# A one-core attention and feed-forward kernel: another prologue, a last group in halves, a second attention buffer and a new written-out order

## The chip, the cores and the metric

The kernel runs on one core of a Trainium2 chip. The metric is the device time of one execution in microseconds (us). A core has five engines with instruction streams of their own: TensorE (PE; its weight loads are listed as PEld), VectorE (DVE), ScalarE (ACT), GpSimd (POOL) and SyncE (SP, which here only issues DMAs). Matmul results land in PSUM, eight banks of 128 partitions by 512 f32 values; everything else is in SBUF.

## What is computed

`x` has 2048 tokens of 640 features. After a layernorm without weights, multi-query attention (32 heads of size 20 that share one key and one value head) and a feed-forward block of width 1728 run on the same normalised input, and both results are added to `x`.

```python
def _A_ref(x, wq, wk, wv, wo):
    q = (lambda x, *d: x.transpose(*d))((x @ wq).reshape(B, S, H, Dh), 0, 2, 1, 3)
    k = x @ wk
    v = x @ wv
    scores = jnp.einsum("bhqd,bkd->bhqk", q, k) * (Dh ** -0.5)
    p = _softmax(scores, axis=-1)
    o = jnp.einsum("bhqk,bkd->bhqd", p, v)
    return (lambda x, *d: x.transpose(*d))(o, 0, 2, 1, 3).reshape(B, S, H * Dh) @ wo

def _B_ref(x, w1, w2):
    h = jnp.einsum("bsd,df->bsf", x, w1)
    h = _silu(h)
    out = jnp.einsum("bsf,fd->bsd", h, w2)
    return out

x = A_x
xn = _layernorm(x, axis=-1)
return x + _A_ref(xn, A_wq, A_wk, A_wv, A_wo) + _B_ref(xn, B_w1, B_w2)
```

## The kernel before, in words

**A planner writes the order.** While the program is built, a class `Sched` (from L170) keeps a modelled clock per engine and commits operations in the order in which they would become ready (`ready` L229, `commit` L254, `run` L279), with priorities for the operations of ACT, DVE, POOL and SP. The result is one fixed in-order list per engine, with semaphores between them; on the chip nothing is reordered. So a constant of the planner (`T_PE`, `SWITCH`, `t_mm` L401 and the like) costs no time itself, but another value gives another order.

**Score blocks.** The work is cut into 2048 score blocks: one 128-token key tile, one head, one chunk of 512 query tokens. There are 4 chunks; a group is 4 heads of one chunk, 64 blocks, 32 groups in all. A block's matmul uses 32 of the 128 rows, so blocks of up to four heads stand side by side in the array. TensorE visits the scores in runs ("S visits", `do_S` L1122, matmul L1152) of mostly three or four blocks, each block into a PSUM bank of its own. The exponential of a block is taken on ScalarE (L1180, one instruction for one to three neighbouring banks) or, for about a third of the blocks, approximated on VectorE by clamped integer arithmetic (`p1` L1197) and two phase-shifted copies, made by VectorE (L1225) or GpSimd (L1231); such a block is then multiplied by three value matrices. The second product ("PV", `do_pv` L1047, matmul L1062) fills one bank, 7, with 32 columns for each of the four heads, four 32-column matmuls to a pass of 512.

**Jobs.** Between score visits and PV passes stand passes of other work: the queries of later heads and chunks (`qd_job` L1313, evicted at L1329 and spread to 32-row slots by 20-row DMAs, L1338), the hidden layer (`h_job` L1350, ACT L1375, DVE L1383) and the output projections (`out_job` L1425). They and PV use the same column-tiled form (`cols` L520, matmul L522); changing between it and a score visit is a change of the array's tiling. Where the planner finds TensorE idle it may put in matmuls of zeros (`fill` L911, matmuls L929 to L952).

**The order around the change.** The first 64 blocks are ordered by the planner's rules (`step` L728); from there the string `ORDER` (L76) says what TensorE does next: `P` a PV pass, `J` a pass of a job, and a letter of `VISITS` a score visit of so many blocks, so many of them for VectorE. What remains after the last score goes by `tail` (L794).

**Prologue** (`prologue`, from L1572). x comes in 16 tiles of 128 tokens on SP's queue (L1588), then the weights; `wk` and `wv` on ACT's queue (L1602). Statistics are taken by VectorE (L1693, L1695) or, for `ACT_STATS`, by ScalarE's accumulator (L1678, L1681). The reciprocal root is a Newton iteration on VectorE (`newton` L1722, L1733 to L1751) in the batches of tiles (0,4), (4,10), (10,16). `norm` (L1711) then applies it on the engine listed. Tiles 0 to 3, 7 and 8 are transposed on TensorE (`tr_job` L1800, matmul L1804; evicted by ACT L1812 or DVE L1815), the ten tiles of `DT` by DMA from SP's queue (L1772). `k_job` (L1819, eviction L1831, shifted copy on POOL L1833) and `v_job` (L1838, three scaled copies L1852) make keys and values for every four tiles; `q_job` (L1290) makes the queries of the first heads for all 512 tokens of chunk 0 in five matmuls (L1295), evicted by ACT at L1303. ScalarE also copies three weights into padded slots (L1664 and twice L1667). A DMA of constants (L1784) fills the offset planes that the queries of the other heads need first.

**End of a group** (`end_group` L1271). VectorE evicts bank 7 (L1274), DMAs transpose it, VectorE takes the reciprocal of the sums (L1258), GpSimd normalises (L1263). When a chunk's heads are there, `try_oT` (L1390) issues DMA transposes into the one buffer `oT`, from which the output jobs read; this waits until the outputs of the chunk before have been evicted. The last group is transposed on TensorE in one piece (L1282, L1411). Of the last chunk's eight output tiles (4 token tiles by 2 halves of 320 columns), four have their first terms summed early and evicted as f32 (`yx`, L1457); for the other four `hold_job` (L1498) keeps the partial sum, with the residual added by multiplying with an identity, in a bank, so that ScalarE can evict the final sum (L1468). VectorE evicts the others with the addition (L1471); the result leaves by DMA (L1475).

## Time and profile before

| | us |
|---|---|
| runs of the kernel before | 683.64, 685.71, 685.64 (median 685.64) |
| the profiled execution, its own time | 685.26 |
| span of that execution in the profile | 683.4 |

The mean clock that TensorE was granted is 0.998 of full speed. The page lists, for each engine, busy time and its share of the span, then the chain of work that ended last, followed back from the last instruction to what released it, then the costliest groups of instructions by line, engine and operation. In a row of the timeline stand start, length, engine, line and operation, output and input with partitions and elements, the number of instructions in the row, and in brackets how long the engine had been idle and what ended that. A row of several instructions covers them all. Matmuls overlap in the pipeline, so a pass costs the distance from one start to the next and not the length shown.

### The profile page before, as it was taken

The numbers are of one execution on the slowest core, as the hardware profiler recorded it, in microseconds if no ns is written. First come the engines' busy times: TensorE is split into PE (matmuls) and PEld (weight loads), VectorE is DVE, ScalarE is ACT, GpSimd is POOL, SyncE is SP. The second block draws the span as 40 slices with busy tenths as digits, with TensorE's granted clock in tenths as the row PEclk, the third lists the DMA queues.
The fourth block names the chain that finished last, engine by engine and source line by source line (L and its number), as shares of the span: only waits on it lengthen the run. The fifth ranks groups of instructions, "written<-read, shape, count | busy, mean of one in ns | idle before, by whom it ended". The sixth has DMA issues, their size and how long they took to land.

```text
span 683.4 us, 22606 instructions
## 1 busy us (share of the span) xinstructions
PE 668.2 (98%) x9667; PEld 228.3 (33%) x9667; DVE 622.1 (91%) x1115; ACT 663.8 (97%) x756; POOL 552.7 (81%) x436
## 2 busy tenths in 40 slices
PE   7899999999999999999999999999999999999997
PEld 3332323333333333333333333333333333333324
DVE  7889989889999989899899999999999999999985
ACT  5999999999999999999999999999999999999995
POOL 3477899987888998898888987878879787788882
PEclk9999999999999999999999999999999999999999
DMA  9546210000021000111112000010112000000012
GB/s 273 149 143 209 65 19 10 11 18 18 17 36 29 10 18 17 29 36 17 30 29 41 13 23 17 29 30 18 29 30 48 9 3 19 19 10 19 20 23 58
DMA packets 52568, 28.00 MB, mean 41 GB/s; under 512 B 38422, under 2 KB 51830, under 8 KB 52470
## 3 DMA queue, kind: packets, MB, share of 16 engines
q1 hardware_dynamic: 51014, 26.35, 15.0%
q8 instruction: 78, 1.28, 0.8%
q10 hardware_dynamic: 1456, 0.22, 0.2%
q14 instruction: 20, 0.16, 0.1%
HBM read 11.44 MB, written 2.62 MB: 21 GB/s over the span
## 4 chain that ended last, share of the span: by engine, by line
PE 86%; DVE 5%; ACT 5%; DMA 3%; issue 1%; SPq 0%; POOL 0%; ACTq 0%
PE psall L1062 30%; PE psall L1152 28%; PE psall L522 27%; ACT sbt L1180 4%; DVE sbt L1197 3%; DMA sbt<-sbt 2%; DMA sbt<-in_A_x_dram 1%; ACT sbt L1713 0%; DVE sbt L1225 0%; DVE sbt L1383 0%; PE psall L1362 0%; PE psall L1295 0%; DVE sbt L1693 0%; PE psall L1804 0%; DVE sbt L1274 0%
## 5 line engine op out<-in xcount | busy, mean ns | idle before, releaser
L1180 ACT ACTIVATE sbt<-psall 128x1024 bf16<-128x1024 f32 (+2 forms) x670 | 627.1, 1040 | 4.1 <-PE psall L1152 3.0
L1231 POOL TENSOR_TENSOR sbt<-sbt 128x768 int32<-128x768 int32 (+1 forms) x368 | 518.6, 1433 | 95.0 <-DVE sbt L1225 82.2
L1197 DVE TENSOR_SCALAR sbt<-psall 128x512 int16<-128x512 f32 x710 | 465.7, 685 | 41.9 <-PE psall L1152 34.9
L1062 PE MATMUL psall<-sbt 128*32 128x512 bf16 x3468 | 279.3, 383 | 0.4 <-DVE sbt L1274 0.4
L1152 PE MATMUL psall<-sbt 32*128 32x512 bf16 x2048 | 252.9, 384 | 4.9 <-DVE sbt L1197 2.2
L522 PE MATMUL psall<-sbt 128*32 128x320 bf16 (+1 forms) x3879 | 235.1, 331 | 1.4 <-DMA sbt<-sbt 1.1
L1152 PEld LDWEIGHTS psall<-sbt 32*128 32x128 bf16 x2048 | 65.5, 91 | 238.2 <-issue 89.0
L522 PEld LDWEIGHTS psall<-sbt 128*32 128x32 bf16 x3879 | 86.7, 95 | 89.4 <-issue 44.0
L1062 PEld LDWEIGHTS psall<-sbt 128*32 128x32 bf16 x3468 | 71.2, 95 | 102.6 <-issue 71.2
L1225 DVE TENSOR_SCALAR sbt<-sbt 128x1536 int16<-128x1536 int16 (+1 forms) x118 | 66.3, 566 | 0.4
L1383 DVE SCALAR_TENSOR_TENSOR sbt<-sbt,psall 128x512 bf16<-128x512 bf16 (+1 forms) x56 | 37.8, 675 | 0.4 <-ACT sbt L1375 0.3
L1375 ACT ACTIVATE sbt<-psall 128x512 bf16<-128x512 f32 x54 | 33.2, 616 | 0.6
L1263 POOL TENSOR_TENSOR sbt<-sbt 128x320 bf16<-128x320 bf16 x31 | 22.5, 727 | 5.3 <-DVE sbt L1225 3.5
L1274 DVE CAST sbt<-psall 128x512 bf16<-128x512 f32 x32 | 21.8, 682 | 0.2 <-PE psall L1062 0.2
L952 PE MATMUL psall<-sbt 128*128 128x512 bf16 (+2 forms) x46 | 13.0, 426 | 1.8 <-DVE sbt L1632 1.2
L1471 DVE SCALAR_TENSOR_TENSOR sbt<-psall,sbt 128x320 bf16<-128x320 f32 x28 | 13.4, 486 | 0.9 <-PE psall L522 0.7
L1833 POOL TENSOR_SCALAR sbt<-sbt 128x256 bf16<-128x256 bf16 x8 | 3.8, 476 | 12.2 <-DVE sbt L1831 11.6
L1329 DVE TENSOR_SCALAR sbt<-psall 128x512 bf16<-128x512 f32 (+1 forms) x19 | 13.0, 683 | 0.3
L1693 DVE BATCH_NORM_STATS2 sbt<-sbt 128x6 f32<-128x320 bf16 x24 | 10.7, 470 | 2.4 <-DMA sbt<-in_A_x_dram 2.4
L1718 POOL TENSOR_SCALAR sbt<-sbt 128x640 bf16<-128x640 bf16 x5 | 4.3, 872 | 7.6 <-DVE sbt L1718 5.4
L1258 DVE RECIPROCAL sbt<-sbt 128x16 f32<-128x16 bf16 x31 | 7.6, 246 | 2.7 <-DMA sbt<-sbt 2.6
L952 PEld LDWEIGHTS psall<-sbt 128*128 128x128 bf16 x46 | 4.5, 108 | 7.8 <-issue 2.4
(70 smaller groups left out, 87.9 us busy)
## 6 DMA issues: line engine op xcount, KB each, us to landing
sbt<-in_A_x_dram SPq DMA_DIRECT2D x32, 160.0 KB, 3.7
out_dram<-sbt SPq DMA_DIRECT2D x15, 160.0 KB, 1.8
sbt<-in_B_w_dram SPq DMA_DIRECT2D x5, 432.0 KB, 6.3
sbt<-sbt SPq DMA_DIRECT2D x105, 20.0 KB
sbt<-in_B_w_dram SPq DMA_DIRECT2D x13, 160.0 KB, 3.0
sbt<-sbt SPq DMA_DIRECT2D x1, 1024.0 KB, 6.4
sbt<-sbt SPq DMA_TRANSPOSE x57, 2.5
sbt<-in_A_wo_dram SPq DMA_DIRECT2D x5, 160.0 KB, 3.0
```

The lines of the kernel that those rows point to most:

```text
L522: ins = pe.matmul(self.bk(b, 0, n, j, j + SLOT), w[:, j:j + SLOT], x, start=start, stop=stop, tile_position=(0, j), skip_group_check=True)
L952: return pe.matmul(self.bk(b, 0, n), self.zero[:, 0:P], self.zero[:, 0:n], start=True, stop=True)
L1062: ins = pe.matmul(self.bk(UBANK, 0, QW, r, r + SLOT), self.v[:, it.w, it.kt, :], it.x(), start=f, stop=False, tile_position=(0, r), skip_g ...
L1152: ins = pe.matmul(self.bk(bank[i]), self.kT[r:r + SLOT, 1 if i in dv else 0, kt * P:(kt + 1) * P], self.qT[r:r + SLOT, g % 8, (g // 8) % 2 ...
L1180: return a.activation(self.E[:, (b0 + lo) * QW:(b0 + lo + m) * QW], self.ps[:, b * BANK:(b + m) * BANK], AF.Exp, scale=ACT_SCALE)
L1197: return v.tensor_scalar(self.Z[:, zs, zp * QW:(zp + 1) * QW], self.bk(bb), 0.0, ZMAX, ALU.max, ALU.min)
L1225: sc.new("dve", td, lambda v, k=k: v.tensor_scalar(self.Y[:, zs, k, 0:w], self.Z[:, zs, 0:w], float(PH[k + 1][0]), None, ALU.add), zk, yk, ...
L1231: sc.new("pool", tp, lambda v, k=k, cb=cb: v.tensor_tensor(self.Y[:, zs, k, 0:w].bitcast(I32), self.Z[:, zs, 0:w].bitcast(I32), cb, ALU.ad ...
L1263: op = sc.new(eng, 0.75 if eng == "pool" else t_dve_ps(16 * DH), lambda v: v.tensor_tensor(dst, ut[:, :, :, 0:DH], rb, ALU.mult), [key, (" ...
L1274: ev = sc.new("dve", t_dve_ps(QW), lambda v: v.tensor_copy(self.U[:, up, :], self.bk(UBANK)), [("UB",)], [("U", up)], prio=U_PRIO, name=f" ...
L1375: sc.new("act", t_act(QW), lambda a: a.activation(t, src, AF.Tanh, scale=0.5), [("B", b)], [("tb", tp)], prio=X_PRIO, name=f"th{c}_{fk}")
L1383: sc.new("dve", t_dve_ps(QW), lambda v, r0=r0, r1=r1, ht=ht: v.scalar_tensor_tensor(out=ht[r0:r1, :], in0=t[r0:r1, :], scalar=1.0, in1=src ...
```

## The change

It has six parts, and lines of the changed kernel are some 10 to 40 off those of before.

1. **Loads.** x tile 1 is loaded from ACT's queue; `wk` and `wv` from SP's, after tiles 0, 2 and 3.
2. **Statistics and norm.** Tiles 0 and 1, and tiles 2 and 3, form two batches whose root is taken by ScalarE's Sqrt and inverted by VectorE; Exp's table is loaded after the second. Newton stays for the batches (4,9) and (9,16). The norm is (x − mean) · rstd; tiles 0 and 2 are normalised by GpSimd, 1 and 3 by VectorE; one tile less is normalised by ScalarE (3 of 16 instead of 4). The statistics that ScalarE takes are those of tiles 7, 8, 9, 14.
3. **Weights and evictions.** The three padded copies move from ScalarE to GpSimd. The evictions of the transposed tiles 0 to 3 are all VectorE's. The queries of the first heads are made by token tile (`q_part`) and evicted in two halves of 256, one by VectorE and one by ScalarE. A `v_job` is evicted by one instruction for the three scalings. The transposes, k and q parts are issued in the order `HEAD`.
4. **Order.** The planner's constants, the earliest times and priorities of prologue operations (`AT`, `PRI`) and the whole string `ORDER` are new; zero matmuls are allowed at a higher busy share in the first 64 steps. The code that could attach single matmul rows to score visits, which was switched off (`RIDE_MIN = 99`), is gone.
5. **Two attention buffers.** Odd chunks' transposes go to the part of `xnT` that held tokens 0 to 511, so that `try_oT` waits for the chunk before the last.
6. **Last group.** Eviction, transpose, reciprocal, normalisation and second transpose each run in two halves of 256 tokens. All eight last output tiles have their partial sums evicted as f32, `hold_job` is gone; three outputs are copied by ScalarE and added by GpSimd, five are added by VectorE; the last token tile's output leaves in two halves, on SP's and ACT's queues.

```diff
-H0_STEP = 24
+H0_STEP = 30
-NEARLY = 2
+BY_ACT = ((0, 0), (0, 1), (2, 0))
-SWITCH = 0.1
-T_PE = 0.2215
+SWITCH = 0.106
+FIRST = 0.01
+T_PE = 0.2165
...
-    "JJJcJGPCJPPbPPPHPCGPJJhJJBJBPPPPPBPKPcPPePHPPMPfbPPPfPPBbPPmBPPbPPBPJbJPbPJJBJPBPJJBJBJJPbJJJJJPPbBP"
+    "hGPPfPPbPPfPPHhbJJgJJJhgPPPPPfPPbPPFPPBPPckPPbkPcPJgPJBJPcJJPHGPPPFPPaJJJBPJJPBFPJJJCJJaJJJJJghPPPPH"
...
-FILL_EARLY = 0.6
+FILL_EARLY = 0.95
-PRO = "v0 t7 t8 v1 k2 k3 q1 k4 k5 v2 k6 k7 d0 v3"
-ACT_STATS = [4, 8, 9, 14]
-NW_ENG = ("dve", "dve", "dve")
-NORM_ENG = ['pool', 'pool', 'pool', 'act', 'act', 'pool', 'dve', 'act', 'dve', 'pool', 'dve', 'act']
-BATCHES = ((0, 4), (4, 10), (10, 16))
+HEAD = "t1 t0 p0 t2 k0 p1 t3 p2 k1 p3"
+Q_ENG = ['dve', 'act']
+W_ENG = ("pool", "pool", "pool")
+X_ENG = ['dve', 'dve', 'dve', 'dve']
+PRO = "t7 v0 t8 v1 k2 k3 q1 k4 k5 k6 v2 k7 d0 v3"
+ACT_STATS = [7, 8, 9, 14]
+NW_ENG = ['sqrt', 'sqrt', 'dve', 'dve']
+NORM0 = ['pool', 'dve', 'pool', 'dve']
+NORM_ENG = ['dve', 'pool', 'pool', 'act', 'pool', 'pool', 'dve', 'act', 'dve', 'pool', 'dve', 'act']
+BATCHES = [[0, 2], [2, 4], [4, 9], [9, 16]]
...
+        for h in (1, 0):
+            c0 = 256 * h
+            ev = sc.new("dve", t_dve_ps(256), lambda v, c0=c0: v.tensor_copy(
+                self.U[:, up, c0:c0 + 256], self.bk(UBANK, c0, c0 + 256)), [("UB",)], [("Uh", h)],
+                prio=U_PRIO + 0.001 * h, name=f"Uev{g}")
...
+    def q_part(self, i):
...
+        half = i // 2
...
+        for k in range(DC):
+            def f(pe, b, k=k):
+                return pe.matmul(self.bk(b, i % 2 * P, i % 2 * P + P), self.wqp[:, k, 0:P],
+                                 self.xnT[:, k, i * P:i * P + P], start=(k == 0), stop=(k == DC - 1))
...
+    def oT_of(self, c):
+        if c % 2:
+            return self.xnT[:, :, 0:QW], [("xnT", i) for i in range(4)]
+        return self.oT[:, :, :], [("oT", i) for i in range(4)]
...
-        if c < 0 or c in self.oT_made or self.norm_made[c] < need or (c > 0 and self.f_done[c - 1] < 8):
+        if c < 0 or c in self.oT_made or self.norm_made[c] < need or (c > 1 and self.f_done[c - 2] < 8):
...
+            if src == "yx" and (i, e) in BY_ACT:
...
+                op = sc.new("act", t_act(320), lambda a: a.activation(half, ps, AF.Copy, scale=0.5), [("B", b)],
+                            [("half", k)], prio=X_PRIO, name=f"out{n}_{e}")
...
+                sc.new("pool", 0.7, lambda g: g.tensor_tensor(ost[:, e0:e0 + 320], half, in1, ALU.add),
+                       [("half", k), rk], wk, prio=X_PRIO, name=f"add{n}_{e}")
...
-        np_("act", t_act(400), wkrep, [("st", "k")], [("wk",)], prio=1.0, name="wkrep")
+        copy(W_ENG[0], *wkrep(), [("st", "k")], [("wk",)], 1.0, "wkrep")
...
+        load_x(0)
+        load_x(1, "act")
+        load_x(2)
+        load_x(3)
...
-                xa(n), self.xslot(n), self.rstd[:, n:n + 1], self.nb[:, n:n + 1], ALU.mult, ALU.add),
+                xa(n), self.xslot(n), self.mv[:, n, 0:1], self.rstd[:, n:n + 1], ALU.subtract, ALU.mult),
...
+            sq = np_("act", 0.22, lambda v: v.activation(v_, self.mv[:, a:b_, 1], AF.Sqrt, bias=self.eps[:, :]),
+                     mvk(a, b_) + [("eps",)], [("va", a)], prio=-1.0, name="sqrt")
+            np_("dve", 0.16, lambda v: v.reciprocal(self.rstd[:, a:b_], v_), [("va", a)], [("rs", a)], prio=-0.1,
+                name=f"rstd{a}")
```

More of the change, by code (lines that the diff above doesn't have):

```diff
@@ L599, in bank_for_job @@
             banks = [b for b in range(7) if b not in hold]
+        banks = [b for b in banks if b not in self.heldb.values()]
         best = None
@@ L1749, in newton @@
                     nw(lambda v: v.tensor_tensor(y_, w_, y_, ALU.mult), rw + rr, rr)
+            if all(eng_of(n) != "act" for n in range(a, b_)):
+                return
             if eng == "dve":
```

418 lines of the change are left out of this document (204 added, 214 removed).

## Prediction

> **What bounds the kernel now.** I read the page first (busy time per engine, then the chain of work that ended last), then the busy time by stage, then single stretches of the timeline.
>
> ```profile
> span 683.4 us, 22606 instructions
> PE 668.2 (98%) x9667; PEld 228.3 (33%) x9667; DVE 622.1 (91%) x1115; ACT 663.8 (97%) x756; POOL 552.7 (81%) x436
> PE 86%; DVE 5%; ACT 5%; DMA 3%; issue 1%; SPq 0%; POOL 0%; ACTq 0%
> ```
>
> TensorE is busy 98% and carries 86% of the final chain; ScalarE, at 97%, is hardly freer. The stages below are cut at the starts of the first score block, the 16th, the 64th and block 1920 of 2048, and at the last exp's end; columns are stage, length, busy time (instructions) of PE, PEld, DVE, ACT, POOL, then clock, DMA share, GB/s.
>
> ```profile
> 0.00:9.95 9.95, 6.65 (x23) 2.55 (x23) 6.37 (x25) 4.93 (x10) 5.39 (x24) 1.00 0.83 229
> 9.95:15.82 5.87, 5.73 (x43) 3.36 (x44) 4.75 (x19) 3.95 (x8) 0.05 (x1) 0.71 1.03 334
> 15.82:27.46 11.64, 8.71 (x87) 3.97 (x85) 10.86 (x48) 11.54 (x17) 4.34 (x6) 1.00 0.59 184
> 27.46:44.53 17.07, 16.51 (x199) 6.61 (x200) 13.72 (x29) 16.29 (x18) 12.27 (x13) 1.00 0.65 182
> 44.53:632.89 588.36, 585.99 (x8689) 195.20 (x8687) 548.07 (x930) 584.97 (x658) 497.38 (x370) 1.00 0.12 29
> 632.89:673.90 41.01, 38.82 (x497) 12.71 (x493) 34.32 (x60) 40.57 (x45) 33.27 (x25) 1.00 0.11 25
> 673.90:683.40 9.50, 5.78 (x144) 3.93 (x139) 4.01 (x10) 1.53 (x4) 0.00 (x0) 1.00 0.20 71
> ```
>
> Each stage has its own limit: before 15.82 a chain of dependences; to 27.46 ScalarE (11.54 of 11.64); from there TensorE, though in the middle ScalarE lies only 1.0 behind it (584.97 against 585.99); from 632.89 ScalarE (40.57 of 41.01); then a chain again. The profiled run took 685.26, 1.86 more than its span; the median of the runs is 685.64. All sums start from 685.26.
>
> **Prologue to the first score block.**
>
> ```profile
> 1.82 1.28 ACT L1757 ACT_TABLE_LOAD   x1 [1.82 <-issue]
> 3.11 0.20 ACT L1757 ACTIVATE sbt<-sbt 128x1 f32<-128x1 f32 x1
> 3.13 1.28 DVE L1693 BATCH_NORM_STATS2 sbt<-sbt 128x6 f32<-128x320 bf16 x3 [2.01 <-DMA sbt<-in_A_x_dram]
> 6.16 0.54 ACT L1667 ACTIVATE sbt<-sbt 128x400 bf16<-128x400 bf16 x1 [2.13 <-DMA sbt<-in_A_wq_dram]
> 7.34 0.17 DVE L1733 TENSOR_SCALAR sbt<-sbt 128x4 f32<-128x4 f32 x1
> 9.41 1.50 DVE L1718 TENSOR_SCALAR sbt<-sbt 128x640 bf16<-128x640 bf16 x4
> 12.37 2.29 PE L1295 MATMUL psall<-sbt 128*128 128x512 bf16 x5
> 15.82 0.60 PE L1152 MATMUL psall<-sbt 32*128 32x512 bf16 x6
> L1713 ACT ACTIVATE sbt<-sbt 128x640 bf16<-128x640 bf16 x4 | 3.5, 914 | 0.0
> L1833 POOL TENSOR_SCALAR sbt<-sbt 128x256 bf16<-128x256 bf16 x8 | 3.8, 476 | 12.2 <-DVE sbt L1831 11.6 <-DVE sbt L1225 0.5
> ```
>
> Before, all four tiles wait for one Newton chain (7.34 to 9.41), the last norm ends at 10.91, and q waits for four transposes and their evictions until 12.37. After, tiles 0 and 1 need only their own statistics: the three statistics from 3.13 to 4.41 set the pace, so the pair is aggregated near 5.5, and root (the nearest row is the one-element activation of 0.20) and reciprocal, each with its hand-over an estimated 0.4, and VectorE's statistics of tile 2 between them put the first norm's end near 7.3. Norms of tiles 0 and 2 stand on GpSimd behind the two pad copies (nearest row: 476 ns for 256 elements; I take 0.6 each), the second of which waits for the weight that ScalarE picks up at 6.16 today: norm 0 ends near 8.2, norm 2 near 9.2. All four transposed-tile evictions now stand on VectorE among the statistics and half of the q parts; placing these in the built order by their rows, tile 3 is evicted near 12.5, the last q part (640 of 2560 columns, a fourth of 2.29) ends near 13.4 and the first score block starts near 14.4: −1.4. Bounds: −0.4, if the VectorE queue slips by two more evictions, to −2.6, if the Newton chain's 2.07 and half a microsecond behind it go entirely. The new table loads cost nothing here: the first takes the old one's place at 1.82, the second (1.28) lies ahead of ScalarE's first statistics, while ScalarE waits for tiles. Loads moved to other queues cost nothing either, as tile 0 keeps its place.
>
> The Trainium skill, "ScalarE: Activation LUTs", section "What ACT_TABLE_LOAD costs", adds a drain of 1.38 us to the 1.28 us load at each change of set. This trace agrees with the load (1.28); behind it the next activation starts at 3.11, 0.01 after its end, so that no drain is seen there, but nothing ran ahead of it, and a change from one set to another is not in the trace.
>
> **From there to block 64.** ScalarE binds and loses a norm (0.91) and a pad copy (0.54): of these and the start, 1.4 + 0.9 + 0.5 = 2.8 could remain. But the second limit is SP's queue:
>
> ```profile
> 26.31 0.17 DVE L1751 SCALAR_TENSOR_TENSOR sbt<-sbt 128x6 f32<-128x6 f32 x1
> 20.20 14.62 SPq L1772 DMA_TRANSPOSE sbt<-sbt  x10
> 34.86 5.98 DMA sbt<-sbt
> 40.88 0.40 PE psall L522 x4
> ```
>
> Ten transposes issue from 20.20 to 34.82, then comes the copy that fills the offset planes of the other heads, on which TensorE waits until 40.88. The last batch's Newton chain ends at 26.48 and six of the ten stand behind it: 8.3, or 1.4 each. After, the batches (with a three-tile lead) let that chain end near 24.5, an estimate from the 1.4 of the start and the norm that ScalarE loses; but tile 9 has moved into the last batch, so seven transposes follow, 9.7, and the copy issues between 34.2 and 34.6 and lands 0.2 to 0.7 earlier than now (5.98 later). Counted in the two built orders, 61 score blocks instead of 55 stand ahead of the first such score: six at 17.07/48 = 0.36 are 2.1 of work, of which I take 1.3 as done in time, for VectorE too is busy 10.86 of 11.64 in the stage before. So the gain at block 64 lies between 0.2 + 1.3 = 1.5 and 2.8; I take **−2.2**, the middle, which holds the start's 1.4. The q and v edits lie inside it: one VectorE instruction in place of three per v part leaves that engine as busy as now, since it takes two more tile evictions.
>
> **The middle.** Nothing is computed less; the order is rewritten. What an alternation costs:
>
> ```profile
> 299.46 0.73 PE L522 MATMUL psall<-sbt 128*32 128x320 bf16 x16
> 300.12 0.39 PE L1152 MATMUL psall<-sbt 32*128 32x512 bf16 x3
> 300.45 0.61 PE L1062 MATMUL psall<-sbt 128*32 128x512 bf16 x8
> 300.99 0.39 PE L1152 MATMUL psall<-sbt 32*128 32x512 bf16 x3
> 301.31 1.05 PE L1062 MATMUL psall<-sbt 128*32 128x512 bf16 x16
> 302.30 0.40 PE L1152 MATMUL psall<-sbt 32*128 32x512 bf16 x4
> 58.88 0.39 PE L1152 MATMUL psall<-sbt 32*128 32x512 bf16 x4
> 59.66 0.39 PE L1152 MATMUL psall<-sbt 32*128 32x512 bf16 x3 [0.38 <-DVE sbt L1197]
> L1180 ACT ACTIVATE sbt<-psall 128x1024 bf16<-128x1024 f32 x570 | 542.0, 1040 | 3.7 <-PE psall L1152 2.8
> L1180 ACT ACTIVATE sbt<-psall 128x1536 bf16<-128x1536 f32 x49 | 71.9, 1479 | 0.2
> L1180 ACT ACTIVATE sbt<-psall 128x512 bf16<-128x512 f32 x51 | 29.8, 620 | 0.3 <-PE psall L1152 0.2
> PEld psall L1152 <- ACT sbt L1180: 48.0, 119, 1.0
> ```
>
> Start to start, four 512-wide passes with their change of shape take 302.30 − 301.31 = 0.99, two take 0.54, so a pass costs 0.225 and a change 0.09; the score visit adds 0.33: 0.42 per visit, be it of three blocks or four. A 320-wide pass costs (0.66 − 0.09)/4 = 0.14. In the built orders, between blocks 64 and 1920, separate visits fall from 567 to 555 (four-block ones rise from 108 to 131, longer ones from 25 to 28): −12 × 0.42 = −5.0. A visit of seven splits in two halves 0.78 apart (58.88 to 59.66) with a 0.38 wait for VectorE, 0.78 more than one visit: three more cost 3 × 0.78 = +2.3. Two 512-wide and four 320-wide passes less: −0.45 − 0.56. Zero matmuls grow from 448 to 1248 columns: 800/512 × 0.225 = +0.35. Sum **−3.4**. Bounds: −5.7 without the cost of the long visits; on the other side ScalarE, which the order does not relieve: 548 two-block, 60 three-block and 63 one-block exps stand for 570, 49 and 51, at the means quoted −22.9 + 16.3 + 7.4 = +0.8, for one block more in all. The second attention buffer lets output transposes be written sooner, hidden already: TensorE is idle for only 588.36 − 585.99 = 2.4 there.
>
> **The end.**
>
> ```profile
> 674.49 0.68 DVE L1274 CAST sbt<-psall 128x512 bf16<-128x512 f32 x1
> 676.01 0.49 DVE L1263 TENSOR_TENSOR sbt<-psall,sbt 128x320 bf16<-128x320 f32 x1
> 678.40 1.68 DVE L1471 SCALAR_TENSOR_TENSOR sbt<-psall,sbt 128x320 bf16<-128x320 f32 x4 [0.72 <-PE psall L522]
> 679.79 0.44 ACT L1468 ACTIVATE sbt<-psall 128x320 bf16<-128x320 f32 x1 [0.43 <-PE psall L522]
> ```
>
> From 632.89 ScalarE binds and its work stays. From the last group's eviction at 674.49 to the last output eviction's end at 680.23 it is 5.74. In halves, the first half's transposes start some 0.3 sooner, but VectorE then has about 14 instructions: two evictions, two reciprocals, two normalisations (about half of 0.68, 0.26, 0.49 plus fixed parts: 2.0 in all), attention copies and five outputs at 0.42 (1.68/4) and partial sums between them; about 5.95. ScalarE's three outputs go on to GpSimd, beside them. **+0.2**, bounds −1.0 (full overlap of the halves) and +0.8 (one GpSimd add last).
>
> **Sum:** −2.2 − 3.4 + 0.2 = −5.4; 685.26 − 5.4 = **679.9**.
>
> **Rivals.** (a) *ScalarE takes the middle's bound.* It lies 1.0 behind TensorE already; if its 0.8 more counts and TensorE's saving is lost in waits, −2.2 + 0.8 + 0.2 = −1.2: 684.1. For it: the windows row. Against: exps wait for scores by only 2.8 in all, and ScalarE's start is earlier. (b) *The start's gain stops at SP's queue:* the copy lands at 40.8 again and blocks fill no gap; the start's 2.2 falls to zero: 682.1. (c) *The early zero matmuls do not hold the clock*, granted 0.71 in the second stage; PE was busy for 6.65 of the first 9.95, and the built order has 37 zero matmuls instead of 25 ahead of the first score. All q parts at half speed would take their 2.29 as now instead of about 1.1, which I have half counted: +1.2, 681.1. (d) *Slower: the longer visits wait for banks.* A four-block visit needs four free banks, and 24 more of them in the whole kernel (120 to 144) each wait for an exp. Place: score weight loads behind the exps, priced at 48.0/119 = 0.40. 24 × 0.40 = +9.6 on −5.4: 689.5. It wipes the gain out from 5.4/24 = 0.23 per visit, and shows as slower from 0.33. For: that wait is the largest with a real releaser. Against: the timeline at 302.30 shows a four-block visit without a wait.
>
> (e) *The table change drains ScalarE as well.* If its second load costs twice its row, statistics on ScalarE slip by 1.4, and of this about 1.0 reaches block 64: 680.9. That is the Trainium skill's rule named above; by its figure the change would cost 2.66.
>
> **How the numbers follow.** Forecast 0.40; (a) 0.15; (b) 0.15; (c) 0.10; (e) 0.05; (d) 0.15. Runs of this kernel tell about 0.3% from no change, that is 683.6 and 687.7. Forecast, (b), (c) and (e) are faster: 0.70; (a) is within: 0.15; (d) slower: 0.15. The range runs from 676.5 (start −2.8 and middle −5.7, with a tail of +0.2, give 677.0, less the half microsecond by which executions differ, 685.26 and 685.64 being two of them) to 686.0, which takes in (a) with the start's lower bound and the tail's +0.8 (−1.4 + 0.8 + 0.8 = +0.2, 685.5) and the same half microsecond; (d) is left out.
>
> **What would show it.** First score block at 14.4 (right) or near 15.5 (VectorE's queue); block 64 at 42.3; blocks 64 to 1920 in 585.0, with TensorE's waits for exps at 48 as now, where (d) needs 57; if ScalarE's busy time fills the middle while PE's falls, it is (a); a granted clock near 0.7 after 10 us is (c); a gap behind the second table load is (e); 5.9 from the last eviction of the group to the last output eviction. The forecast is wrong if visits saved are paid back by waits, which the total of these waits tells.

## The result, and the profile after

The changed kernel is slower: 693.9 us median (692.96 to 694.83, four runs) against 684.85 for the kernel before in the same sessions; the ratio is 1.0133, 95% interval 1.0110 to 1.0157. The forecast was 679.9, with a range to 686.0. The profiled execution took 693.66, its span is 691.5, and so 8.1 longer than that of before.

The page of the changed kernel, in the order in which the forecast read it:

```profile
span 691.5 us, 22597 instructions
PE 670.0 (97%) x9666; PEld 229.5 (33%) x9669; DVE 624.0 (90%) x1108; ACT 661.7 (96%) x754; POOL 572.8 (83%) x453
PE 72%; ACT 12%; DVE 8%; DMA 4%; POOL 2%; issue 1%; DVEq 0%
PE psall L1033 25%; PE psall L1119 23%; PE psall L527 22%; ACT sbt L1142 12%; DMA sbt<-sbt 4%; DVE sbt L1159 4%; POOL sbt L1715 2%; DVE sbt L1690 1%; DVE sbt L1187 1%; DVE sbt L1237 0%; PE psall L940 0%; DMA sbt<-in_A_x_dram 0%; PE psall L1366 0%; PE psall L1850 0%; DVE sbt L1481 0%
```

Only one engine's busy time grew by much: GpSimd, 552.7 to 572.8; seven norms of 2.50 in place of five of 0.87 are 13.1 of these 20.1. And a line of GpSimd, the norm (L1715), has come into the final chain with 2% of the span, some 14 us. The busy time by stage, with the edges at the same blocks as before (first, 16th, 64th, 1920th, last exp's end). In this table the block edges lie 0.08 ahead of the starts in the timeline; in later tables they lie up to 0.24 beside them, by the same amount at both ends of a stage. The text gives a block's start as the timeline has it:

```profile
0.00:17.29 17.29, 14.16 (x86) 7.20 (x87) 11.69 (x40) 8.43 (x18) 12.47 (x33) 1.00 0.87 253
17.29:33.51 16.22, 10.31 (x92) 4.91 (x92) 10.25 (x46) 11.18 (x15) 10.43 (x5) 0.79 0.39 114
33.51:52.07 18.56, 16.94 (x177) 6.38 (x178) 12.76 (x24) 15.95 (x19) 12.70 (x13) 0.90 0.75 177
52.07:640.15 588.08, 583.04 (x8673) 194.64 (x8669) 547.63 (x927) 583.70 (x660) 499.03 (x374) 1.00 0.12 29
640.15:681.76 41.61, 39.96 (x523) 13.25 (x519) 35.09 (x59) 41.30 (x43) 35.70 (x27) 1.00 0.16 25
681.76:691.50 9.74, 5.59 (x131) 3.17 (x124) 6.57 (x19) 1.09 (x3) 2.51 (x3) 1.00 0.20 69
```

Block 64 comes at 52.15 instead of 44.53: +7.6, nearly the whole loss. In the second row's stage no engine is near its limit (ScalarE leads with 11.18 of 16.22; GpSimd spends 10.43 on five instructions), which is what a chain of waits looks like. From block 64 to 1920 the stage is 0.28 shorter: TensorE is busy 2.95 less, and idle 2.67 more. The rest is +0.5 up to the last exp's end and +0.24 behind it.

Four of the five instructions are norms, the fifth is a pad copy of 0.52. First the norms of before in the view of their line (minimum, median, maximum in ns), then GpSimd's timeline and TensorE's of the changed kernel:

```profile
L1718 POOL TENSOR_SCALAR sbt<-sbt x5: 868/875/875, 19.3 to 28.1; 128x640 bf16<-128x640 bf16 x5
```

```profile
7.79 4.99 POOL L1715 TENSOR_SCALAR sbt<-sbt 128x640 bf16<-128x640 bf16 x2 [0.29 <-DVE sbt L1692]
19.89 4.98 POOL L1715 TENSOR_SCALAR sbt<-sbt 128x640 bf16<-128x640 bf16 x2 [2.70 <-DVE sbt L1715]
25.30 2.50 POOL L1715 TENSOR_SCALAR sbt<-sbt 128x640 bf16<-128x640 bf16 x1
30.89 2.50 POOL L1715 TENSOR_SCALAR sbt<-sbt 128x640 bf16<-128x640 bf16 x1 [3.08 <-DVE sbt L1753]
```

```profile
10.35 0.45 PE L1831 MATMUL psall<-sbt 128*128 128x128 bf16 x5 [1.00 <-POOL sbt L1715]
12.83 0.45 PE L1831 MATMUL psall<-sbt 128*128 128x128 bf16 x5 [0.89 <-POOL sbt L1715]
17.36 0.60 PE L1119 MATMUL psall<-sbt 32*128 32x512 bf16 x6
27.86 0.71 PE L1831 MATMUL psall<-sbt 128*128 128x128 bf16 x5 [4.37 <-POOL sbt L1715]
```

A GpSimd norm takes 2.50 us, where the norm of before took 0.87 on the same 128x640 tile. TensorE's transposes of tiles 0, 2 and 8 wait for it, the last for 4.37; behind that wait, transposes that took 0.44 take 0.71: the clock granted in the stage is 0.79.

### The profile page after: what moved, and what is told of

The parts are those of the page before. It is cut to its first block, busy times and chain, and to the rows that moved or that the text cites. A ratio compares the mean times of both kernels' runs of the same rounds, so it can differ in the third digit from the quotient of the medians.

```text
span 691.5 us, 22597 instructions
## 1 busy us (share of the span) xinstructions
PE 670.0 (97%) x9666; PEld 229.5 (33%) x9669; DVE 624.0 (90%) x1108; ACT 661.7 (96%) x754; POOL 572.8 (83%) x453
## 4 chain that ended last, share of the span: by engine, by line
PE 72%; ACT 12%; DVE 8%; DMA 4%; POOL 2%; issue 1%; DVEq 0%
PE psall L1033 25%; PE psall L1119 23%; PE psall L527 22%; ACT sbt L1142 12%; DMA sbt<-sbt 4%; DVE sbt L1159 4%; POOL sbt L1715 2%; DVE sbt L1690 1%; DVE sbt L1187 1%; DVE sbt L1237 0%; PE psall L940 0%; DMA sbt<-in_A_x_dram 0%; PE psall L1366 0%; PE psall L1850 0%; DVE sbt L1481 0%
## 5 line engine op out<-in xcount | busy, mean ns | idle before, releaser
L1193 POOL TENSOR_TENSOR sbt<-sbt 128x768 int32<-128x768 int32 (+2 forms) x374 | 521.6, 1420 | 91.5 <-DVE sbt L1187 79.2
L1119 PE MATMUL psall<-sbt 32*128 32x512 bf16 x2048 | 250.3, 385 | 6.1 <-DVE sbt L1159 2.3
L527 PE MATMUL psall<-sbt 128*32 128x320 bf16 (+1 forms) x3847 | 231.0, 331 | 1.1 <-DVE sbt L1462 1.1
L527 PEld LDWEIGHTS psall<-sbt 128*32 128x32 bf16 x3847 | 85.2, 95 | 90.6 <-issue 46.0
L1033 PEld LDWEIGHTS psall<-sbt 128*32 128x32 bf16 x3466 | 70.1, 95 | 101.0 <-issue 68.9
L1187 DVE TENSOR_SCALAR sbt<-sbt 128x1536 int16<-128x1536 int16 (+2 forms) x116 | 65.5, 571 | 0.7
L1715 POOL TENSOR_SCALAR sbt<-sbt 128x640 bf16<-128x640 bf16 x7 | 17.5, 2500 | 6.1 <-DVE sbt L1753 3.1
L953 PE MATMUL psall<-sbt 128*128 128x512 bf16 (+5 forms) x56 | 16.6, 440 | 1.7 <-DVE sbt L1624 1.2
L1842 DVE COPY sbt<-psall 128x640 bf16<-128x640 bf16 x6 | 2.9, 487 | 6.8 <-PE psall L1831 6.8
```

Source lines behind the costliest of these rows:

```text
L527: ins = pe.matmul(self.bk(b, 0, n, j, j + SLOT), w[:, j:j + SLOT], x, start=start, stop=stop, tile_position=(0, j), skip_group_check=True)
L1033: ins = pe.matmul(self.bk(UBANK, 0, QW, r, r + SLOT), self.v[:, it.w, it.kt, :], it.x(), start=f, stop=False, tile_position=(0, r), skip_g ...
L1119: ins = pe.matmul(self.bk(bank[i]), self.kT[r:r + SLOT, 1 if i in dv else 0, kt * P:(kt + 1) * P], self.qT[r:r + SLOT, g % 8, (g // 8) % 2 ...
L1187: sc.new("dve", td, lambda v, k=k: v.tensor_scalar(self.Y[:, zs, k, 0:w], self.Z[:, zs, 0:w], float(PH[k + 1][0]), None, ALU.add), zk, yk, ...
L1193: sc.new("pool", tp, lambda v, k=k, cb=cb: v.tensor_tensor(self.Y[:, zs, k, 0:w].bitcast(I32), self.Z[:, zs, 0:w].bitcast(I32), cb, ALU.ad ...
L1715: np_(eng, 0.36 if eng == "dve" else 0.87, lambda v: v.tensor_scalar(xa(n), self.xslot(n), self.mv[:, n, 0:1], self.rstd[:, n:n + 1], ALU. ...
```

## Theories

**Theory 1**: the form of the norm. Before, GpSimd computed x · rstd + (−mean · rstd), operations multiply and add; the change computes (x − mean) · rstd, operations subtract and multiply. **Rival**: VectorE's queue, which has taken four evictions, or the moved loads, make the start late, and the long norms lie in time that was idle. For the middle: either the new order's own waits ate its saving, or the late start disturbed it.

## The experiments

"Before" stands beside every result with the runs of the same session (median 684.3 to 684.7).

**The norm's form alone.** In the changed kernel, norms on GpSimd only:

```diff
+            if eng == "pool":
...
+                    xa(n), self.xslot(n), self.rstd[:, n:n + 1], self.nb[:, n:n + 1], ALU.mult, ALU.add),
...
+                out=self.nb[:, a:b_], in0=self.mv[:, a:b_, 0], scalar=-1.0, in1=self.rstd[:, a:b_], op0=ALU.mult,
```

> The changed kernel with one edit: GpSimd's norms are taken as x * rstd + (-mean * rstd), as before the change; VectorE makes the four extra -mean * rstd. Theory 1 (the form): a GpSimd norm as (x - mean) * rstd took 2.50 us for 0.87, and this carries the loss up to block 64. Then the seven norms take 0.87 each, the first score block comes near 14.9 instead of 17.36, block 64 near 43.5 to 45 instead of 52.1, and the time falls by 7 to 9 us, to 685 to 687. Rival (VectorE's queue): the norms get shorter, but TensorE then waits for VectorE's evictions and statistics; block 64 stays above 49 and the time above 690.

Measured: 719.6, ratio 1.0514 (1.0498 to 1.0529). The start did what Theory 1 said: first score block at 14.77, block 64 at 44.84. But the stage behind it took 619.11:

```profile
44.80:663.91 619.11, 603.41 (x8766) 205.54 (x8767) 553.32 (x933) 594.90 (x683) 496.68 (x375) 1.00 0.11 27
```

Four small VectorE instructions had moved the planner's clock, so that at token 117 of the written order a score visit found no room; from there the planner put in PV passes of its own and the string ran out of step with the work (94 zero matmuls in the middle instead of 5, counted in the built program). The total says nothing on the norm. This is a finding of its own: the string `ORDER` fits one prologue.

**The order kept.** The negated mean is made by small VectorE instructions that the planner is told take no time; the norm is then add and multiply. The order on TensorE, ScalarE, GpSimd and SP is the changed kernel's to the instruction.

```diff
+            if eng == "pool":
...
+                np_("dve", 0.0, lambda v: v.tensor_scalar(nm, self.mv[:, n, 0:1], -1.0, None, ALU.mult), [("mv", n)],
+                    [("nm", n)], prio=-0.2, name=f"nm{n}")
...
+                    xa(n), self.xslot(n), nm, self.rstd[:, n:n + 1], ALU.add, ALU.mult),
```

> The changed kernel with GpSimd's norms as (x + (-mean)) * rstd; seven small VectorE instructions make -mean, planned at no time, so that the order on TensorE, ScalarE, GpSimd and SP is that of the changed kernel to the instruction (the first experiment changed it everywhere behind block 64). Theory 1 (the form costs the start): GpSimd's norms take 0.87, first score block near 14.8, block 64 near 44.8 as in the first experiment, and the time is 7 below the changed kernel's 693.9. Within that, if the new order's own waits ate its saving, blocks 64 to 1920 take 588 again and the time is 686 to 687; if the late start had disturbed them, they take 585 and the time is 683 to 684. Rival (VectorE's queue binds the start): time above 690.

Measured: 688.87, 5.0 below the changed kernel; ratio to before 1.0067 (1.0051 to 1.0082), where the changed kernel had 1.0133, which makes 4.5 of it. The seven norms take 0.876 (the view of one line: minimum, median, maximum in ns):

```profile
L1720 POOL TENSOR_SCALAR sbt<-sbt x7: 871/876/884, 7.9 to 30.0; 128x640 bf16<-128x640 bf16 x7
```

First score block 14.90, block 64 at 46.50. So the form is worth 4.5 to 5, and not the 7 expected: something else still holds the start. Up to the first score block it is VectorE, as the rival said: the chain of work runs over VectorE without a wait from 3.81 to 15.3 (statistics, norms, evictions). The middle took 587.95, so the late start had not been what held it; and 2.9 of this execution's 688.8 lie around its span of 685.9, 1.0 more than before's 1.86 (medians of all executions: 2.76 and 1.88).

**The form put into the kernel before.**

```diff
+            if eng == "pool":
...
+                    xa(n), self.xslot(n), self.mv[:, n, 0:1], self.rstd[:, n:n + 1], ALU.subtract, ALU.mult),
```

> The kernel before with one edit: its five GpSimd norms (tiles 4, 5, 6, 9, 13) as (x - mean) * rstd. Theory 1: each takes 2.5 instead of 0.87 here too; three in a row delay the DMA transposes of tiles 4 to 6 by 1.6, 3.3 and 4.9, and block 64 comes 3 to 5 later; time 688 to 690. Rival: the form is slow only beside the changed kernel's other traffic, or off the path; then the time is within 1 us of before.

Measured: 690.34, ratio 1.0079 (1.0064 to 1.0095), +5.6. Four norms in a row took 9.95 (3.44 before), and block 64 came at 49.04, 4.5 later than in before's profile and 5.8 to 6.0 later than in two other kernels with the same prologue (e4_before_order 43.00, e5_before_new_order 43.29):

```profile
17.91 9.95 POOL L1719 TENSOR_SCALAR sbt<-sbt 128x640 bf16<-128x640 bf16 x4 [2.20 <-DVE sbt L1756]
30.95 2.50 POOL L1719 TENSOR_SCALAR sbt<-sbt 128x640 bf16<-128x640 bf16 x1 [3.09 <-DVE sbt L1723]
```

Theory 1 holds in both kernels.

**Which part of the form.** Five tiles, five forms, on the first experiment's kernel.

```diff
+                if n == 2:
...
+                    go(r, ALU.mult, w1, ALU.subtract, k)
+                elif n == 5:
...
+                    go(w1, ALU.add, r, ALU.mult, k)
+                elif n == 6:
+                    go(m, ALU.subtract, r, ALU.mult)
+                elif n in (8, 9):
+                    s1, o1, s2, o2 = (m, ALU.subtract, r, ALU.mult) if n == 8 else (r, ALU.mult, b, ALU.add)
...
+                else:
+                    go(r, ALU.mult, b, ALU.add)
```

> The first experiment's kernel, with another form of the norm on GpSimd for five tiles: tile 2 multiply then subtract, tile 5 add then multiply, tile 6 subtract then multiply (as the change has it), tile 8 two instructions (subtract alone, multiply alone), tile 9 two instructions (multiply alone, add alone); tiles 0 and 13 multiply then add. If the subtraction is what is slow: tiles 2, 6 and 8's first at about 2.5 or above 1.5, all others 0.9 or below. If it is an addition or subtraction in the first place: 5 and 6 at 2.5, 2 at 0.87. If it is only the pair in that order with a mean from a strided column: 6 alone.

GpSimd's timeline of that kernel: L1721 holds the pairs (tiles 0, 2, then 5 and 6, then 13), L1733 and L1735 the single operations.

```profile
7.86 0.87 POOL L1721 TENSOR_SCALAR sbt<-sbt 128x640 bf16<-128x640 bf16 x1 [0.37 <-DVE sbt L1692]
10.44 2.50 POOL L1721 TENSOR_SCALAR sbt<-sbt 128x640 bf16<-128x640 bf16 x1 [1.72 <-DVE sbt L1724]
18.28 1.89 POOL L1733 TENSOR_SCALAR sbt<-sbt 128x640 bf16<-128x640 bf16 x1 [3.24 <-DVE sbt L1778]
20.26 1.89 POOL L1735 TENSOR_SCALAR sbt<-sbt 128x640 bf16<-128x640 bf16 x1
22.59 0.87 POOL L1721 TENSOR_SCALAR sbt<-sbt 128x640 bf16<-128x640 bf16 x1
23.91 2.50 POOL L1721 TENSOR_SCALAR sbt<-sbt 128x640 bf16<-128x640 bf16 x1
```

Multiply and subtract (tile 2) takes 2.50 like subtract and multiply; multiply and add takes 0.87, add and multiply too (0.876 in the experiment above). So within a pair it is the subtraction, in either place; tiles 2 and 5 take their scalars from the same two places and differ, so where a scalar lies is not the cause. Unexpected: a single operation, be it multiply, add or subtract, takes 1.89, more than twice the pair of multiply and add; why is open. One execution took 691.02.

**The loads.** With the form mended, TensorE still waited: in that kernel (e8_same_plan) a v job waits 2.71 for the DMA transposes of tiles 4 to 6; of the ten transposes the slowest lands 7.1 after its issue, the median 2.5.

```profile
25.82 0.34 PE L1879 MATMUL psall<-sbt 128*128 128x20 bf16 x7 [2.71 <-DMA sbt<-sbt]
DMA to landing us min/median/max: 2.4/2.5/7.1
```

Three kernels undo the change's loads, all of them (e15_old_loads) or one half each (below, the first pair of lines is e17_x1_sp's, the second e18_kv_act's):

```diff
-        load_x(1, "act")
+        load_x(1)
...
-            load_w("sp", k, [lambda q, sv=sv, j=j: q.dma_start(self.kv_st[:, j, :, :], sv)], ("st", k), 25600)
+            load_w("act", k, [lambda q, sv=sv, j=j: q.dma_start(self.kv_st[:, j, :, :], sv)], ("st", k), 25600)
```

> As e8_same_plan, but with the loads of before: all x tiles on SP's queue, wk and wv on ScalarE's. If the two weight loads on SP's queue delay what is issued behind them, x tiles 4 to 15 and w1 are issued 1 us earlier, the transposes of tiles 4 to 6 land 1 earlier, TensorE's wait of 2.7 at 23 to 26 us shrinks, and block 64 and the time come 1 to 2 earlier. Rival: the first norm comes later as tile 1 does, the time is the same or up to 1 longer.

Measured: 684.83, ratio 1.0004 (0.9991 to 1.0018): 4.0 below the mended kernel, and no longer apart from before. Its profiled execution was one of its longer ones (686.65): the v job's wait is 0.43 there, but a later wait for a transpose takes 1.59 and block 64 comes only at 46.33, so for block 64 the next kernels speak.

> As e8_same_plan, but x tile 1 on SP's queue between tiles 0 and 2; wk and wv stay on SP's. If the tile on ScalarE's queue was the cost, the time falls by 3 to 4 to about 685; if the weights on SP's queue were, it rises by up to 0.5, since everything behind is issued 0.4 later still.

Measured: 688.53, ratio 1.0052 (1.0031 to 1.0072): no gain, and the first transpose still lands after 6.6, so tile 1's queue is not the cost.

> As e8_same_plan, but wk and wv on ScalarE's queue behind x tile 1; tiles 0, 2 and 3 stay on SP's. If the weights on SP's queue were the cost (x tiles 4 to 15 and w1 issued 1.1 to 1.5 later), the time falls by 3 to 4 to about 685; if tile 1 on ScalarE's queue was, it stays near 688.5.

Measured: 685.91, ratio 1.0024 (1.0007 to 1.0040): 3.0 below the mended kernel. The weights on SP's queue were the cost. The 4.0 and the 3.0 differ outside the profile: the median span falls from 686.1 to 683.3 here and to 683.05 with all loads undone, but what lies around the span is 2.55 here and 1.80 there. Why is open; e1_mul_add had the change's loads and 1.78. SP's timeline, of the mended kernel and then of this one, with a view of the transposes and the v job's wait of this one:

```profile
2.12 0.44 SPq L1597 DMA_DIRECT2D sbt<-in_A_wk_dram  x1
2.60 0.53 SPq L1597 DMA_DIRECT2D sbt<-in_A_wv_dram  x1
3.17 1.15 SPq L1599 DMA_DIRECT2D sbt<-in_A_wq_dram  x1
4.36 5.75 SPq L1579 DMA_DIRECT2D sbt<-in_A_x_dram  x12
12.52 2.57 SPq L1604 DMA_DIRECT2D sbt<-in_B_w_dram  x5
```

```profile
2.12 0.43 SPq L1599 DMA_DIRECT2D sbt<-in_A_wq_dram  x1
2.60 5.75 SPq L1579 DMA_DIRECT2D sbt<-in_A_x_dram  x12
10.77 2.38 SPq L1604 DMA_DIRECT2D sbt<-in_B_w_dram  x5
DMA to landing us min/median/max: 2.4/2.5/3.6
23.56 0.65 PE L1879 MATMUL psall<-sbt 128*128 128x20 bf16 x20 [0.36 <-DMA sbt<-sbt]
```

Two issues of half a microsecond, and a third that takes 1.15 for 0.43 behind them, put every later load 1.75 back: w1 is issued until 15.1 instead of 13.2, and the first transposes, issued near 17.5 in both kernels, land in up to 7.1 behind it and in 3.6 without. The v job's wait falls from 2.71 to 0.36, and block 64 comes at 43.73 instead of 46.50 (44.13 in e19_loads_out, with all loads undone, below). What the transposes wait for can be read from the landings: w1's last load lands at 24.03 in the mended kernel and at 20.54 in this one, the first transpose at 24.57 and 21.12. In 16 of the 18 profiles it lands 0.53 to 0.79 behind w1's last load; in the other two, before and e2_before_sub, it is issued at 20.2 and 20.4, takes 2.5, and w1 has landed 1.5 and 2.0 ahead of it. Why w1 lands 3.5 later for an issue 1.75 later is only argued: the DMA engines were busier (share 0.84 from 16 to 30 us in the mended kernel, 0.60 in this one). Of the 2.8 at block 64, this profiled execution keeps 1.0 at the span's end (684.9 for 685.9): its middle took 589.6.

**The zero matmuls.** All early ones 64 columns wide:

```diff
+        n = 64 if now < 17.0 else n
```

> As e8_same_plan, but every zero matmul ahead of 17 us of the planner's clock is 64 columns wide instead of up to 512: same places, less work. If the early zero matmuls hold TensorE's clock, the granted clock falls to 0.6 to 0.7 between 9 and 17 us, transposes and q parts take twice as long, and the time is 1 to 2 above e8_same_plan's. Rival: the clock stays at 1.00 without them and the time is the same within 0.5.

Measured: 687.93, ratio 1.0051 (1.0032 to 1.0071): not slower than the mended kernel. TensorE did run slowly without them, which the length of a tile's five transposes tells (0.44 at full speed), though the clock column says 1.00:

```profile
10.53 0.74 PE L1841 MATMUL psall<-sbt 128*128 128x128 bf16 x5
12.29 0.44 PE L1841 MATMUL psall<-sbt 128*128 128x128 bf16 x5
15.32 0.60 PE L1121 MATMUL psall<-sbt 32*128 32x512 bf16 x6
```

The first score block came at 15.32 for 14.90 in the mended kernel, and there the chain does pass over the slow matmuls from 10.03 to 12.49. But that is 0.4 and not the 1.2 of rival (c), and at block 64 nothing of it is left (45.54 for 46.50).

**The second buffer.** One buffer, with the old condition:

```diff
-        if c % 2:
+        if False:
...
-        if c < 0 or c in self.oT_made or self.norm_made[c] < need or (c > 1 and self.f_done[c - 2] < 8):
+        if c < 0 or c in self.oT_made or self.norm_made[c] < need or (c > 0 and self.f_done[c - 1] < 8):
```

> As e8_same_plan, but with one attention buffer, whose transposes wait for the outputs of the chunk before, as before the change; TensorE's order is the same. If the second buffer takes waits away, the time is 1 to 3 above e8_same_plan's; by the forecast (hidden already) it is the same within 0.5.

Measured: 689.17, ratio 1.0057 (1.0038 to 1.0076): no difference. TensorE's order is the same with it and without.

**The order in the kernel before**, first as it stands:

```diff
-    "JJJcJGPCJPPbPPPHPCGPJJhJJBJBPPPPPBPKPcPPePHPPMPfbPPPfPPBbPPmBPPbPPBPJbJPbPJJBJPBPJJBJBJJPbJJJJJPPbBP"
+    "hGPPfPPbPPfPPHhbJJgJJJhgPPPPPfPPbPPFPPBPPckPPbkPcPJgPJBJPcJJPHGPPPFPPaJJJBPJJPBFPJJJCJJaJJJJJghPPPPH"
...
```

> The kernel before with the changed kernel's written order from block 64 on, all else of before. Theory 1 (the forecast's count): 12 score visits fewer save 3 us where the stages ahead are undisturbed, so blocks 64 to 1920 take 585 and the time is 681 to 682. Rival (waits for banks): the longer visits wait; TensorE is busy 2 to 3 less and idle 2 to 3 more, the stage takes 588 and the time is 684 to 687.

Measured: 716.7, ratio 1.0475 (1.0457 to 1.0492): out of step at token 117, as in the first experiment, since the string starts at block 70 and the kernel before stands at 67. Then with one more visit of three blocks ahead of it:

```diff
-    "hGPPfPPbPPfPPHhbJJgJJJhgPPPPPfPPbPPFPPBPPckPPbkPcPJgPJBJPcJJPHGPPPFPPaJJJBPJJPBFPJJJCJJaJJJJJghPPPPH"
+    "bhGPPfPPbPPfPPHhbJJgJJJhgPPPPPfPPbPPFPPBPPckPPbkPcPJgPJBJPcJJPHGPPPFPPaJJJBPJJPBFPJJJCJJaJJJJJghPPPP"
```

> The kernel before with the changed kernel's written order behind one more three-block visit (its string starts at block 70 and not 67), so that it is followed but for one place near block 1792, unlike in the fourth experiment. Everything else is of before. If the forecast's count is right, blocks 64 to 1920 take 585 and the time is 681 to 682. Rival (the new order's waits): TensorE is busy 3 less there and idle 3 more, 588, and the time is 684 to 686.

Measured: 690.66, ratio 1.0087 (1.0073 to 1.0102). Blocks 64 to 1500 took 458.5 against 455.1 in before's profile, with TensorE and ScalarE equally busy (585.6 and 585.7 of 594.11 to block 1920). The order saves nothing here. Of the 5.8 lost up to block 1920, 4.1 are there at block 1750, so at most 1.7 belong to the place near block 1792 where it is not followed. The string was written for another prologue, so what it costs by itself is not settled.

**What binds the middle.** Both on the mended kernel, both leaving work out:

```diff
-                return a.activation(self.E[:, (b0 + lo) * QW:(b0 + lo + m) * QW], self.ps[:, b * BANK:(b + m) * BANK],
+                return a.activation(self.E[:, (b0 + lo) * QW:(b0 + lo + m) * QW - c],
+                                    self.ps[:, b * BANK:(b + m) * BANK - c],
```

> As e8_same_plan, but 593 of the exponentials between blocks 80 and 1900 leave out their last 32 columns (stale values stay there), so that ScalarE has 593 x 27 ns = 16 us less to do; TensorE's work and order are the same. Rival (a) of the forecast (ScalarE sets the pace of the middle as much as TensorE): the stage from block 64 to 1920 falls from 588 to about 583, TensorE's busy time there, by its idle 5. If TensorE alone binds, it stays at 588 within 0.7. Either way not below 583.

```diff
+        n = QW - (32 if not any(first) and 80 < self.b_next < 1900 else 0)
...
-                ins = pe.matmul(self.bk(UBANK, 0, QW, r, r + SLOT), self.v[:, it.w, it.kt, :], it.x(), start=f, stop=False,
+                ins = pe.matmul(self.bk(UBANK, 0, n, r, r + SLOT), self.v[:, it.w, it.kt, :], it.x()[:, 0:n], start=f, stop=False,
```

> As e8_same_plan, but some 746 PV passes between blocks 80 and 1900 leave out the last 32 of their 512 columns, 13 ns each, so that TensorE has 10 us less to do; ScalarE's work and order are the same. If TensorE alone binds the middle (the forecast), the stage falls from 588 to about 578. If ScalarE (busy 584 of it) binds as much, it stays above 585.

Measured: 686.97 (ratio 1.0034, 1.0019 to 1.0048) with shorter exps, 684.57 (1.0000, 0.9989 to 1.0011) with shorter passes. The stage from block 64 to 1920, of the mended kernel, with shorter exps and with shorter passes, each in the view of its own kernel:

```profile
46.74:634.69 587.95, 582.94 (x8673) 194.66 (x8670) 547.54 (x927) 583.89 (x660) 499.13 (x374) 1.00 0.12 29
```

```profile
45.69:632.86 587.17, 582.35 (x8677) 193.76 (x8669) 547.86 (x927) 578.46 (x660) 499.13 (x374) 1.00 0.12 29
```

```profile
45.31:630.74 585.43, 578.02 (x8673) 196.72 (x8670) 548.33 (x926) 581.45 (x660) 498.89 (x374) 1.00 0.12 29
```

ScalarE busy 5.4 less (an estimated 593 exps × 27 ns = 16 of work) shortens the stage by 0.8; TensorE busy 4.9 less (an estimated 746 passes × 13 ns = 9.9 of work) by 2.5. The first result fits a stage that TensorE alone binds, the second one that ScalarE binds as much; together they say that neither alone sets the pace. In this fixed order what one engine saves turns into idle time of its own (ScalarE's grows from 4.1 to 8.7, TensorE's from 5.0 to 7.4), and a quarter of TensorE's saving reaches the stage. Both shortened at once was not tried. The whole times fall by more, 1.9 and 4.3, but 0.6 and 1.4 of it lie ahead of block 64 (45.86 and 45.12 for 46.50), where nothing was edited.

**The end.** The last tile's output in one DMA:

```diff
-            if sl == 3:
+            if False:
...
-                op = sc.dma("sp", lambda q: q.dma_start(self.outv[:, n, :], ost),
+                op = sc.dma("act" if sl == 3 else "sp", lambda q: q.dma_start(self.outv[:, n, :], ost),
```

> As e8_same_plan, but the last token tile's output leaves in one DMA from ScalarE's queue, as before the change. If the halves help, the time is 0.5 to 0.7 longer (2.5 from the last eviction to the span's end in the changed kernel, 3.2 before); if the second queue costs at the end of the program what it saves, the time is the same or shorter, and what lies around the span falls from 2.9 to 1.9.

Measured: 687.69, ratio 1.0041 (1.0024 to 1.0057), 1.2 below the mended kernel. But the end is not where it gains: the span ends 2.40 behind the last eviction with one DMA and 2.49 with two, and what lies around the span stays at 2.50, against the expected 1.9. Together with the loads of before:

> The first mended version (norms as add and multiply), the loads of before and one output DMA for the last tile together. The parts gave 5.0, 4.0 and 1.2 on the changed kernel; if they add up, the time is 683.5 to 684, 0.5 below the kernel before at best; if the last two overlap, it is that of before.

Measured: 685.60, ratio 1.0011 (0.9998 to 1.0023), 0.8 above the kernel with the loads of before alone. The two differ in sign: the halves are worth less than these comparisons can tell, and what is left of the change, mended, does not beat the kernel before.

**The kernel before with four more zero matmuls.**

```diff
+        if self.nfill == 22:
+            op.mm = 5
+            one = op.fn
+            op.fn = lambda pe: [one(pe) for _ in range(5)][-1]
```

> The kernel before with four more zero matmuls behind its first 23, ahead of the first transpose; all else the same. In its profiled execution the zeros ended at 7.84, TensorE sat idle for 2.1, the granted clock was 0.64 between 10 and 14 us and the first score block came at 15.8; in executions of the same prologue where they ended at 8.75 it was 1.00 and 14.4. If the gap is what lowers the clock, the profile shows 1.00 and a first score block at 14.3 to 14.6, and the time falls by 0.5 to 1.5; if not, it stays within 0.3 or rises by the 0.9 that the zeros take.

Measured: 684.04, ratio 0.9986 (0.9974 to 0.9999). Its clock between 9.95 and 14.20 was 1.00, where before's profile had 0.64; but e4_before_order, with the prologue of before and no more zeros, had 1.00 too. Before, e4_before_order and this kernel:

```profile
9.95:14.20 4.25, 4.11 (x27) 2.14 (x28) 4.18 (x15) 2.89 (x6) 0.00 (x0) 0.64 1.05 325
9.95:14.20 4.25, 3.59 (x35) 2.44 (x35) 4.18 (x16) 3.77 (x8) 0.00 (x0) 1.00 1.06 325
9.95:14.20 4.25, 3.40 (x32) 2.29 (x33) 4.25 (x16) 3.16 (x7) 0.00 (x0) 1.00 1.01 338
```

So one profile cannot show that the zeros hold the clock. What speaks for it is that the slowest of 12 runs is 684.71 where before's slowest of 29 is 687.20. The first score block came at 14.99, not 14.3 to 14.6, as the first transpose waited for its norm until 10.20 in this execution. It is the fastest version tried, by half a microsecond that the interval just separates from none.

## Why the prediction was wrong, point by point

- **Start, −2.2 forecast, +7.6 measured.** Two costs failed. The GpSimd norms 0 and 2 were put at 1.0 each ("norm 0 ends near 8.2, norm 2 near 9.2") near the old row, though the change writes another formula; no row showed that one, and it was not bounded. They take 2.50: 5.0 in medians, shown by e8_same_plan and the reverse e2_before_sub. And "loads moved to other queues cost nothing either, as tile 0 keeps its place" looked at the first tile and not at what stood behind on SP's queue: 3.0 to 4.0, shown by e18_kv_act and e15_old_loads. 5.0 + 4.0 is the whole loss of 9.0, in this order of mending: in the changed kernel itself the first transpose is issued only at 19.81 and lands in 3.2, so the loads' cost hides behind the norms until these are mended.
- **The 1.4 of the first score block** was a gain over one execution. Before's profiled execution had the low clock in its second stage; three other kernels with the same prologue, e4_before_order, e2_before_sub and e5_before_new_order, reached the first score block at 14.4 to 14.6, in the time forecast for the change. The mended kernels came to 14.8 to 15.8: VectorE's queue, which the forecast had as its worse bound, takes what the earlier norms give.
- **Pads, root, table.** GpSimd's pad copies took 0.5 (taken as 0.6), the roots 0.29. The second table load and what follows it, in the changed kernel:

```profile
8.13 1.28 ACT L1769 ACT_TABLE_LOAD   x1
9.43 0.20 ACT L1769 ACTIVATE sbt<-sbt 128x1 f32<-128x1 f32 x1
```

  The next activation starts 0.02 after the load's end. The rule of the Trainium skill weighed in the forecast, "ScalarE: Activation LUTs", section "What ACT_TABLE_LOAD costs", adds 1.38 us of drain at a change of set; this change of set, from Sqrt to Exp 0.02 behind the second root, shows none, and rival (e) falls.
- **SP's queue** was rightly named as the second limit, but with the wrong cause: the last seven transposes were issued from 33.4, not from about 25. The last batch's Newton chain ended at 30.8 instead of 24.5, as VectorE had waited 4.56 for tile 8's transposes, which waited for GpSimd's norm.
- **Middle, −3.4 forecast, −0.28 measured.** The count was nearly right: TensorE's busy time fell by 2.95. The step that failed is the last one, that a saving of TensorE's busy time is one of the stage: of the 2.95, 0.28 reached it, and in e14_short_pv 2.5 of 9.9. Rival (a) named the engine beside it, but its 0.8 more of exps is not there (ScalarE is busy 1.27 less in the stage), and ScalarE alone does not bind either (e13_short_exp).
- **Rival (d)**, the slower one, gave 689.5, nearer to the 693.9 than any other, by a mechanism that is not the one at work: luck. Waits of score weight loads for exps did grow, as counted over the whole kernel, but by 7.0, and the stage did not lengthen:

```profile
PEld psall L1119 <- ACT sbt L1142: 55.0, 135, 1.1
```

- **End, +0.2 forecast, +0.24 from the last eviction of the group on.** The size came out by two errors that cancel. VectorE's chain is 6.68 (682.35 to 689.03), not 5.95:

```profile
682.35 0.76 DVE L1245 CAST sbt<-psall 128x256 bf16<-128x256 f32 x2 [0.22 <-PE psall L1033]
686.96 1.07 DVE L1462 SCALAR_TENSOR_TENSOR sbt<-psall,sbt 128x320 f32<-128x320 f32 x2
687.49 0.32 PE L527 MATMUL psall<-sbt 128*32 128x320 bf16 x4 [0.78 <-DVE sbt L1462]
687.95 1.08 DVE L1481 SCALAR_TENSOR_TENSOR sbt<-psall,sbt 128x320 bf16<-128x320 f32 x2
```

  Two partial sums are evicted at 686.96, behind final outputs, and TensorE waits 0.78 for them. The output's last DMA then ends the span 2.47 behind the last eviction instead of 3.17; the split of that output is not the reason, as e10_one_out has 2.40 without it.

## What to carry to other kernels

Price an instruction by a row with its operations, not only its engine and shape: the same tile on the same engine cost 0.87 or 2.50 by one operation. When an issue is added to a queue, follow everything behind it to the first reader, not just the transfer that was in view. And where two engines' busy times are both within 1% of a stage's length, count a saving on one at a fraction until an experiment shortens that engine's work alone; a written order that was searched for one prologue must be searched again when the prologue moves.

## What the runs showed of the hardware

- GpSimd's two-operation tensor-scalar on 128x640 bf16: 0.87 for multiply and add in either order, 2.50 with a subtraction in either place, 1.89 for one operation alone. VectorE took 0.44 for the norm in both forms.
- The first DMA transpose on SP's queue never landed earlier than 0.53 us behind the last of w1's loads from that queue: 0.53 to 0.79 behind it in 16 of 18 profiles, in which it took 3.15 to 7.1 us from its issue instead of 2.5.
- The granted clock between 10 and 14 us was 0.64 in the execution where TensorE's zeros ended 2.1 before the next matmul, and 1.00 in three others where the gap was 0.85 to 1.54 (e4_before_order, e16_before_zeros, e2_before_sub); that the gap is the cause is not shown. In e6_thin_zeros, with 64-column zeros and a gap of 5.3, transposes took 0.69 to 0.74 up to 11 us while the column said 1.00. So a stage's clock is read from the length of a known matmul as well.
